# A linear-attention and gated-FF kernel: a list scheduler orders all of it, Q's maxima of four pairs of heads move to TensorE, and the first phase's FF works on 512 tokens

## The chip, the core and the metric

The kernel runs on one core of a Trainium2 chip. The time is the device's time of one execution, in microseconds (us); several executions are run and their median is given. A core has five engines that are told apart in the profile: PE (TensorE, matrix products into PSUM), DVE (VectorE), ACT (ScalarE), POOL (GpSimd) and SP, which here only issues DMAs. Each works through its own instructions in order and waits on semaphores for the others. PSUM has eight banks of 128 partitions x 512 float32.

## What is computed

```python
def phi(x):
    proj = einsum('bhsd,df->bhsf', x, w_phi)             # 64 -> 128 features
    proj = proj - max(abs(proj), axis=-1)                # one maximum per token
    return concatenate([exp(proj), exp(-proj)], -1)      # 256 features
q_p, k_p = phi(q), phi(k)                                # q, k, v: 8 x 8 x 576 x 64
kv  = einsum('bhsf,bhsd->bhfd', k_p, v)
z   = sum(k_p, axis=2)
att = einsum('bhsf,bhfd->bhsd', q_p, kv) / (einsum('bhsf,bhf->bhs', q_p, z) + 1e-6)
x   = att as [4608 tokens, 512]
out = (sigmoid(x @ w_gate) * (x @ w_val)) @ w_out        # 512 -> 1536 -> 512
```

All is float32. The FF's weights come as float64 bit patterns, and the kernel splits each operand of the FF in a high and a low part in a reduced format that TensorE takes at full rate (float32r); a product is then three matmuls, high by high, high by low and low by high. The attention's matmuls are in plain float32.

## The kernel before, in words

**Attention.** The work is cut in 32 pairs of heads (8 batches, 4 pairs each); a pair fills the 128 partitions with two heads of 64. For a pair, `k_heads` (L427) makes K's features token-major (pk), with a tail of 64 tokens of both heads in a matmul of its own (`rest`, L488). `k_exp` takes the maximum per token on DVE (mx, L438), subtracts it (dk, L451) and lets ACT take both exponentials (ek, L460). `q_half` (L417) makes Q's features feature-major (pq), ACT copies them to d (L479), and `q_max` finds each token's maximum across partitions on DVE: a reduction with a transposition (pm, L506), an exchange between the four partition groups in copies of 36 columns (L511 to L517), a transposition back (mb, L519) and the subtraction (L524). `q_exp` takes the exponentials (L568, L570). `kv` (L534, L548) makes K^T V and the sums z with matmuls whose output is cut in four column groups of 32; z's sum over tokens is on PE up to pair 9 and mostly on DVE from pair 10 on (ONPE = 10, L473, L474). `turn` transposes the result (tp, L560), `num` makes numerator and denominator (nm L584, dp L597). The denominator is gathered in a compact form, inverted, sent to memory and comes back broadcast (dn, den, rb); for the last pair of the first batch it is inverted in place instead (L606, L607). `scale` multiplies (xp, L638) and stores x in a scratch in DRAM (xs).

**First phase of the FF.** While attention runs, the FF's first four of twelve blocks of 128 hidden features (JA = 4) are done on chunks of 256 tokens (CH = 256): `half` makes one product of 12 matmuls (gv, L165), `gate` the sigmoid times the value on ACT and DVE, `half_out` the output products (acc, L172), whose sum is parked in DRAM (ys). The four blocks' weights, twelve tiles, are converted once, by `weight_tile` (L134 to L144), with a second load of the same words shifted by two bytes (wmid). x has two buffers of 256 tokens.

**Second phase of the FF.** `rest_chunks` takes the other eight blocks on chunks of 512 tokens (g, v: L165 and acc: L172), with `load_weights` converting 24 weight tiles on the way, four of the blocks into the space that attention leaves and four into the first phase's weight space, and adds the parked sum.

**Order.** In the first phase the order of all engines is written out by hand: a loop over pairs calls the steps, generators (`start`, `tick`) advance DVE's and ACT's steps a bit at a time, and `fill` adds FF products at a given rate (RATE, LAG, AHEAD, TICKS). `grant` lets the weight tiles go: one for each of the first pairs, then three for each. In the second phase PE's order is written and the framework orders the rest.

Of the kernel before, what the change touches and what calls it, by code (L numbers as in the profile page):

```python
# [28 lines left out]
CH = 256  # L29
NCHUNK = NT // CH  # L30
CW = 512
HS = S // 2
Q = 32

JA = 4
JR = 8
EARLY = NP
ONPE = 10
RATE = 2.8
LAG = (4, 8)  # L40
AHEAD = 3
TICKS = 3
# [3 lines left out]
def attention_moe(  # L46
    ctx: ExitStack,
    tc: tile.TileContext,
    q: bass.AP,
    k: bass.AP,  # L50
# [6 lines left out]
    vec, act, pool = nc.vector, nc.scalar, nc.gpsimd  # L57
# [4 lines left out]
    def split(h, l, x):  # L62
        a = act.copy(h, x)  # L63
        return a, vec.tensor_tensor(l, x, h.bitcast(F32), op=ALU.subtract)

    def behind(stack, marks):
        for m in marks:
            stack.enter_context(tc.issue_after(m.ins))


    weights = {}

    ebias = const.tile([P, 1], F32, name="ebias")
    vec.memset(ebias, -896.0 * 2.0**23)

    def from_f64(h, l, raw, sp, nb, name):

        words = raw.rearrange("p (n two) -> p n two", two=2)
        lo, hi = words[:, :, 0], words[:, :, 1]
        top = sp.tile([P, DM], U32, tag="wtop", name="wtop" + name, bufs=nb)  # L80
        vec.tensor_scalar(top, hi, 0x7FFFFE00, None, op0=ALU.bitwise_and)
        relu = act.activation(top, top, AF.Relu, bias=ebias, scale=8.0)
        vec.scalar_tensor_tensor(
            top, hi, 0x80000000, top, op0=ALU.bitwise_and, op1=ALU.bitwise_or
        )
        nc.sync.dma_start(h.bitcast(U32), top)
        rest, unit = hi, lo
        vec.tensor_scalar(
            hi, hi, 16, 0x01FF0000, op0=ALU.logical_shift_left, op1=ALU.bitwise_and
        )  # L90
        vec.scalar_tensor_tensor(
            hi, lo, 16, hi, op0=ALU.logical_shift_right, op1=ALU.bitwise_or
        )
        vec.tensor_scalar(unit, top, 0xFF800000, None, op0=ALU.bitwise_and)
        return relu, vec.scalar_tensor_tensor(
            l, rest, 2.0**-36, unit.bitcast(F32), op0=ALU.mult, op1=ALU.mult
        )

    def load_weights(j, m, wp, sp, nb):
        if m == 0:  # L100
            wh = wp.tile([P, 3 * DM], F32R, tag=f"wh{j}", name=f"wh{j}")
            wl = wp.tile([P, 3 * DM], F32R, tag=f"wl{j}", name=f"wl{j}")
            weights[j] = (wh, wl)
        wh, wl = weights[j]
        ms = slice(m * DM, m * DM + DM)
        raw = sp.tile([P, 2 * DM], U32, tag="wraw", name=f"wraw{j}_{m}", bufs=nb + 1)
        load = nc.sync.dma_start(raw, w_moe[j, :, m, :].bitcast(U32))
        return load, *from_f64(wh[:, ms], wl[:, ms], raw, sp, nb, f"{j}_{m}")

    def raw_tile(w, sp):  # L110

        j, m = divmod(w, 3)
        raw = sp.tile([P, 2 * DM], U32, tag="wraw", name=f"wraw{j}_{m}")
        nc.sync.dma_start(raw, w_moe[j, :, m, :].bitcast(U32))
        mid = sp.tile([P, 2 * DM], U32, tag="wmid", name=f"wmid{j}_{m}")
        nc.sync.dma_start(
            mid[:, : 2 * DM - 1].bitcast(U16),
            w_moe[j, :, m, :].bitcast(U16)[:, 1 : 4 * DM - 1],
        )
        return raw, mid  # L120

    def weight_tile(w, raw, mid, wp, sp):
        j, m = divmod(w, 3)
        n = f"{j}_{m}"
        if m == 0:
            weights[j] = tuple(
                wp.tile([P, 3 * DM], F32R, tag=f"w{x}{j}", name=f"w{x}{j}") for x in "hl"
            )
        h, l = (x[:, m * DM : m * DM + DM] for x in weights[j])
        hi = raw.rearrange("p (n two) -> p n two", two=2)[:, :, 1]  # L130
        words = mid.rearrange("p (n two) -> p n two", two=2)
        rest, unit = words[:, :, 0], words[:, :, 1]
        top = sp.tile([P, DM], U32, tag="wtop", name="wtop" + n)
        vec.tensor_scalar(top, hi, 0x7FFFFE00, None, op0=ALU.bitwise_and)  # L134
        act.activation(top, top, AF.Relu, bias=ebias, scale=8.0)
        vec.tensor_scalar(rest, rest, 0x01FFFFFF, None, op0=ALU.bitwise_and)
        yield
        vec.scalar_tensor_tensor(
            top, hi, 0x80000000, top, op0=ALU.bitwise_and, op1=ALU.bitwise_or
        )  # L140
        nc.sync.dma_start(h.bitcast(U32), top)
        yield
        vec.tensor_scalar(unit, top, 0xFF800000, None, op0=ALU.bitwise_and)
        vec.scalar_tensor_tensor(  # L144
            l, rest, 2.0**-36, unit.bitcast(F32), op0=ALU.mult, op1=ALU.mult
        )

    xscr, yscr = [], []
    for c in range(NCHUNK):
        xscr.append(dram.tile([P, NC4 * CH], F32, tag=f"xs{c}", name=f"xs{c}"))  # L150
        yscr.append(dram.tile([2, P, DM], F32, tag=f"ys{c}", name=f"ys{c}"))

    def x_tiles(mp, w, name):
        xh = mp.tile([P, NC4 * w], F32R, tag="xh", name="xh" + name)
        xl = mp.tile([P, NC4 * w], F32R, tag="xl", name="xl" + name)
        return xh, xl, xl.bitcast(F32)

    def mm_in(o, xs, j, m, w):
        (xh, xl), (wh, wl) = xs, weights[j]
        i = 0  # L160
        for cc in range(NC4):
            ws = slice(m * DM + cc * P, m * DM + cc * P + P)
            cs = slice(cc * w, cc * w + w)
            for a, x in ((wh, xh), (wh, xl), (wl, xh)):
                nc.tensor.matmul(o, a[:, ws], x[:, cs], start=i == 0, stop=i == 11)  # L165
                i += 1

    def mm_out(acc, t, hs, j, first, last):
        (hh, hl, _), (wh, wl) = hs, weights[j]
        ts, ws = slice(t * P, t * P + P), slice(2 * DM, 3 * DM)  # L170
        for i, (a, w) in enumerate(((hh, wh), (hh, wl), (hl, wh))):
            nc.tensor.matmul(  # L172
                acc, a[:, ts], w[:, ws], start=first and i == 0, stop=last and i == 2
            )

    def gated(g, vl, w, mp, hb, name):
        u = mp.tile([P, w], F32, tag="u", name="u" + name)
        t = mp.tile([P, w], F32, tag="t", name="t" + name)
        hh = mp.tile([P, w], F32R, tag="hh", name="hh" + name, bufs=hb)
        hl = mp.tile([P, w], F32R, tag="hl", name="hl" + name, bufs=hb)  # L180
        act.activation(t, g, AF.Tanh, scale=0.5)  # L181
        act.activation(u, g, AF.Exp)
        tu = t.bitcast(U32)
        vec.tensor_scalar(tu, tu, 0x7FFFFFFF, None, op0=ALU.bitwise_and)  # L184
        vec.scalar_tensor_tensor(t, t, 1.0, vl, op0=ALU.add, op1=ALU.mult)  # L185
        vec.scalar_tensor_tensor(u, u, 1.0, t, op0=ALU.min, op1=ALU.mult)  # L186
        return hh, hl, split(hh, hl, u)

    tasks = []

    def start(g):

        if next(g, tasks) is not tasks:
            tasks.append(g)

    def tick():
        for g in list(tasks):
            if next(g, tasks) is tasks:
                tasks.remove(g)

    def half_units(js, mp, ps_gv, ps_acc, need):
        xs, hs, gvs, parts = {}, {}, {}, collections.Counter()

        def load_x(c):
            xh, xl, raw = x_tiles(mp, CH, f"1_{c}")
            xs[c] = xh, xl
            nc.sync.dma_start(raw, xscr[c])
            for _ in range(3):
                yield
            act.copy(xh, raw)  # L210
            yield
            vec.tensor_tensor(xl, raw, xh.bitcast(F32), op=ALU.subtract)  # L212
            parts[c] = NP

        def begin(c):
            free = c < 2 or parts["v", c - 2] == len(js)
            if c not in xs and free and parts["x", c] == CH * NP:
                start(load_x(c))

        def gate(c, i, n):  # L220
            gv = gvs.pop((c, i))
            u = mp.tile([P, CH], F32, tag="u", name="u" + n)
            t = mp.tile([P, CH], F32, tag="t", name="t" + n)
            hh = mp.tile([P, CH], F32R, tag="hh", name="hh" + n, bufs=10)
            hl = mp.tile([P, CH], F32R, tag="hl", name="hl" + n, bufs=10)
            hs[c, i] = hh, hl, None
# [13 lines left out]
        def half(c, i, m):  # L240
            while parts[c] < NP:
                begin(c)
                tick()
# [109 lines left out]
    with ExitStack() as actx:  # L353
# [442 lines left out]
        while tasks:  # L796
            tick()
# [73 lines left out]
```

## Time and profile before

| | |
|---|---|
| median of 3 runs | 1292.52 us (1292.35 to 1294.36) |
| profiled execution, first to last instruction | 1291.7 us |
| busy: PE, its weight loads, DVE, ACT | 1234.4, 971.2, 786.1, 528.1 us |
| matmul records on PE | 9264 |
| mean granted TensorE clock | 0.973 |
| moved by DMA | 131.56 MB |

The page gives the span of the profiled execution and no other time of it; the span lies 0.8 us under the median of the runs. In the rows that are shown below, a group has its line, engine and operation, the tiles written and read, and a count (x32), then the busy time in all and the mean in ns of one, then the idle time before it and what ended it. A float32 matmul is recorded twice, once for each pass. Matmuls are pipelined, so the duration of one overlaps with the next, and the view of the chain, where each piece lasts until the next one begins, tells better what it costs.

### The profile page before, as it was taken

The numbers are of one execution on the slowest core, as the hardware profiler recorded it, in microseconds if no ns is written. First come the engines' busy times: TensorE is split into PE (matmuls) and PEld (weight loads), VectorE is DVE, ScalarE is ACT, GpSimd is POOL, SyncE is SP. The second block draws the span as 40 slices with busy tenths as digits, with TensorE's granted clock in tenths as the row PEclk, the third lists the DMA queues.
The fourth block names the chain that finished last, engine by engine and source line by source line (L and its number), as shares of the span: only waits on it lengthen the run. The fifth ranks groups of instructions, "written<-read, shape, count | busy, mean of one in ns | idle before, by whom it ended". The sixth has DMA issues, their size and how long they took to land.

```text
span 1291.7 us, 22705 instructions
## 1 busy us (share of the span) xinstructions
PE 1234.4 (96%) x9264; PEld 971.2 (75%) x9264; DVE 786.1 (61%) x1584; ACT 528.1 (41%) x1081; POOL 0.7 (0%) x6
## 2 busy tenths in 40 slices
PE   7767999999999999999889999999999999999998
PEld 5434677777777777777778888888888888888886
DVE  6779778888878778883895953434243434333333
ACT  4635556665655566563443422212222212222221
POOL 0000000000000000000000000000000000000000
PEclk8877899999999999999899999999999999999999
DMA  4448434343433334332754520202020111111010
GB/s 176 153 145 284 136 104 146 111 132 105 127 119 121 99 98 146 98 104 73 270 195 148 195 98 1 95 3 76 22 61 37 58 40 53 46 41 57 6 61 33
DMA packets 80868, 131.56 MB, mean 102 GB/s; under 512 B 18300, under 2 KB 37884, under 8 KB 80764
## 3 DMA queue, kind: packets, MB, share of 16 engines
q1 hardware_dynamic: 80764, 130.11, 31.4%
q8 instruction: 73, 1.20, 0.4%
q14 instruction: 31, 0.25, 0.1%
HBM read 92.04 MB, written 28.45 MB: 93 GB/s over the span
## 4 chain that ended last, share of the span: by engine, by line
PE 86%; DVE 7%; DMA 3%; ACT 2%; issue 1%; SPq 0%; DVEq 0%
PE acc L172 22%; PE g L165 15%; PE v L165 15%; PE gv L165 13%; PE kvz L534 6%; PE nm L584 4%; PE pq L417 3%; PE dp L597 2%; PE pk L427 2%; PE kvz L548 1%; DMA wraw<-w_moe 1%; PE pk L488 1%; ACT ek L460 1%; PE tp L560 1%; DMA rb<-den 1%
## 5 line engine op out<-in xcount | busy, mean ns | idle before, releaser
L165 PE MATMUL gv<-xh,wh 128*128 128x256 f32 x576 | 171.6, 298 | 4.9 <-ACT xh L210 2.6
L172 PE MATMUL acc<-wh,hh 128*128 128x512 f32 x432 | 172.4, 399 | 3.2 <-ACT hh L235 2.5
L172 PE MATMUL acc<-wh,hl 128*128 128x512 f32 x432 | 169.0, 391 | 0.7 <-DVE hl L237 0.7
L172 PE MATMUL acc<-wl,hh 128*128 128x512 f32 x432 | 169.1, 391 | 0.0
L165 PE MATMUL gv<-xl,wh 128*128 128x256 f32 x576 | 164.5, 286 | 2.8 <-DVE xl L212 2.8
L165 PE MATMUL gv<-xh,wl 128*128 128x256 f32 x576 | 164.3, 285 | 0.0
L63 ACT CAST hh<-u 128x512 fp32r<-128x512 f32 x72 | 44.7, 621 | 229.0 <-DVE u L186 229.0
L184 DVE TENSOR_SCALAR t<-t 128x512 uint32<-128x512 uint32 x72 | 30.7, 426 | 166.9 <-ACT t L181 166.7
L165 PEld LDWEIGHTS gv<-xh,wh 128*128 128x128 f32 x576 | 111.5, 194 | 22.7 <-issue 15.7
L181 ACT ACTIVATE t<-g 128x512 f32<-128x512 f32 x72 | 43.0, 598 | 178.5 <-PE g L165 178.4
L165 PEld LDWEIGHTS gv<-xl,wh 128*128 128x128 f32 x576 | 111.7, 194 | 3.5 <-DVE xl L212 3.0
L165 PE MATMUL g<-xh,wh 128*128 128x512 f32 x288 | 113.0, 392 | 0.0
L165 PE MATMUL v<-xh,wh 128*128 128x512 f32 x288 | 112.6, 391 | 0.0
L165 PE MATMUL g<-xh,wl 128*128 128x512 f32 x288 | 112.5, 391 | 0.0
L165 PE MATMUL g<-xl,wh 128*128 128x512 f32 x288 | 112.5, 391 | 0.0
L165 PE MATMUL v<-xl,wh 128*128 128x512 f32 x288 | 112.3, 390 | 0.0
L165 PE MATMUL v<-xh,wl 128*128 128x512 f32 x288 | 112.1, 389 | 0.0
L165 PEld LDWEIGHTS gv<-xh,wl 128*128 128x128 f32 x576 | 111.5, 194 | 0.0
L185 DVE SCALAR_TENSOR_TENSOR t<-t,v 128x512 f32<-128x512 f32 x72 | 49.4, 686 | 97.3 <-PE v L165 97.3
L172 PEld LDWEIGHTS acc<-wh,hh 128*128 128x128 f32 x432 | 81.1, 188 | 27.3 <-issue 6.2
L172 PEld LDWEIGHTS acc<-wh,hl 128*128 128x128 f32 x432 | 81.1, 188 | 20.2 <-DVE hl L237 1.7
L534 PE MATMUL kvz<-ek,v 128*32 128x256 f32 x1280 | 89.6, 433 | 6.8 <-issue 5.8
(97 smaller groups left out, 2141.1 us busy)
## 6 DMA issues: line engine op xcount, KB each, us to landing
wraw<-w_moe SPq DMA_DIRECT2D x36, 512.0 KB
xl<-xs SPq DMA_DIRECT2D x34, 512.0 KB
k<-k SPq DMA_DIRECT2D x32, 320.0 KB
v<-v SPq DMA_DIRECT2D x32, 320.0 KB
q<-q SPq DMA_DIRECT2D x32, 288.0 KB
wh<-wtop SPq DMA_DIRECT2D x36, 256.0 KB
ys<-y SPq DMA_DIRECT2D x36, 256.0 KB
yp<-ys SPq DMA_DIRECT2D x36, 256.0 KB
```

The source lines that it names most:

```text
L63: a = act.copy(h, x)
L165: nc.tensor.matmul(o, a[:, ws], x[:, cs], start=i == 0, stop=i == 11)
L172: nc.tensor.matmul(acc, a[:, ts], w[:, ws], start=first and i == 0, stop=last and i == 2)
L181: act.activation(t, g, AF.Tanh, scale=0.5)
L184: vec.tensor_scalar(tu, tu, 0x7FFFFFFF, None, op0=ALU.bitwise_and)
L185: vec.scalar_tensor_tensor(t, t, 1.0, vl, op0=ALU.add, op1=ALU.mult)
L417: nc.tensor.matmul(pps[hd], wk[head(hd), :], x[head(hd), cs], start=True, stop=True)
L427: nc.tensor.matmul(pps[hd][:, t, :], kx[head(hd), t * P : t * P + P], wk[head(hd), :], start=True, stop=True,)
L460: act.activation(e[:, :, sg * F : sg * F + F], dk, AF.Exp, scale=1.0 - 2.0 * sg)
L534: nc.tensor.matmul(kvz[o : o + Q, : 2 * F], vx[:, 2 * t + hd, o % D : o % D + Q], (e0, e1)[hd][:, t, :] if t < 4 else e2[:, 0, :], start=t ...
L584: nc.tensor.matmul(nms[hf][o : o + Q, :], w[:, sg, o : o + Q], es[sg][:, o // D, cs], start=sg == 0, stop=sg == 1, tile_position=(0, o),)
L597: nc.tensor.matmul(dp[o : o + Q, :], w[:, 2, z : z + Q], es[sg][:, hd, hf * HS : hf * HS + HS], start=sg == 0, stop=sg == 1, tile_position ...
```

## The change

**A list scheduler orders the whole kernel.** Each step becomes an operation (`Op`) with its engine, an estimated duration, a rank (an intended time) and the buffers that it reads and writes. `Plan.run` simulates the engines with these durations. Among the operations of an engine that can start at nearly the same time it takes the lowest rank; on PE an operation that would change the tiling mode (r: rows halved, c: columns in four, f: the full array) has 4 added to its rank. Buffers are rings of slots that are handed out in this order; DMAs are simulated as one wire. The steps are then issued, on every engine, in the order of the simulated times.

```diff
+NQ = 4
+ONPE = 16
+BANKS = 5
+PERIOD = 18.4
+START = 56.0
+LEAD = 90.0
+STICK = 4.0
...
+class Plan:
...
+    SWITCH = 0.15
+    NEAR = {"PE": 0.3, "DVE": 0.05, "ACT": 0.05, "SP": 0.0, "X": 0.0}
...
+                first = min(t for t, _ in ts) + self.NEAR[e]
+
+                def key(x):
+                    t, o = x
+                    off = e == "PE" and mode not in (None, o.mode[0])
+                    return o.rank + STICK * off, t
+
+                t, o = min((x for x in ts if x[0] <= first), key=key)
...
+    def due(i):
+        return 11.0 * i if i < NP else START + PERIOD * (i - NP)
```

A pair's operations have ranks from `due(i)` on; the products of a chunk come 90 (LEAD) behind the pairs that complete it, the gate's steps before all else (rank -100). The twelve weight tiles have ranks from 24 to 82 and keep their conversion.

**Maxima of Q on TensorE.** For the first four pairs Q is loaded with its tail laid out as K's. Its features are made twice: token-major, for the maxima (two reductions on DVE, as K's), and feature-major into PSUM, where the maxima are subtracted by matmuls with a broadcast column against a negated identity; ACT takes the exponentials straight from PSUM.

```diff
+        if on_pe:
+            qt = [bank([P, 4, F]) for _ in range(2)]
+            pe("r", 0.9, lambda: token_major(qt, qx), [qx], qt, r + 0.7, slack)
+            mq = [at(f"mq{g}", 2, [P, 4]) for g in range(2)]
+            for g in range(2):
+                dve(4 * F, lambda g=g: maxima(mq[g](), qt[g](), 4), [qt[g]], [mq[g]], r + 7 + g)
+            qf = [bank([P, DM]), bank([P, DM]), bank([P, 2, TAIL])]
+
+            def project():
+                for hd in range(2):
+                    nc.tensor.matmul(
+                        qf[hd](), wk[head(hd), :], qx()[head(hd), :DM],
+                        start=True, stop=False,
+                    )
+
+            def lower():
+                for hd in range(2):
+                    for t in range(4):
+                        nc.tensor.matmul(
+                            qf[hd]()[:, t * P : t * P + P],
+                            mq[hd]()[:, t : t + 1].broadcast_to([P, P]), minus,
+                            start=False, stop=t == 3,
+                        )
+                tail = qf[2]().rearrange("p a b -> p (a b)")
+                nc.tensor.matmul(tail, wk, qx()[:, DM:], start=True, stop=False)
+                nc.tensor.matmul(
+                    tail, mk[2]()[:, 1:2].broadcast_to([P, P]), minus,
+                    start=False, stop=True,
+                )
```

**FF of the first phase on 512 tokens.** Nine chunks of 512 replace eighteen of 256; a product is 12 matmuls of 512 columns. x is kept in four slots of one feature block each, one set in the first phase. Chunk 0, whose x comes straight from attention, has its products cut by feature block (`parted`), so that a block can be multiplied when its pair is done. The gate's and the output's steps are the same on twice the width.

```diff
-CH = 256
...
+    r_xh, r_xl = (ring(ff, f"x{a}", NC4, CW, F32R) for a in "hl")
...
+        for m, o in enumerate((g, vl)):
+            cuts = range(NC4) if parted else (0,)
+            for c0 in cuts:
+                c1 = c0 + 1 if parted else NC4
+                pe(
+                    "f", 0.683 * (c1 - c0),
+                    lambda o=o, m=m, c0=c0, c1=c1: product(o, m, c0, c1),
...
+        banks = [r_g] if c < NCH - 2 else [r_g, r_a]
```

**The rest.** The sums of ones stay on PE up to pair 15 (ONPE = 16). K's shifted features are written into the place of their second exponential instead of a tile of their own. PSUM is five banks for attention and three for the FF, shared in the first four pairs, in the last two chunks of the first phase and in the second phase. In the second phase the same products, conversions and outputs are done, with x in two sets and everything ordered by the planner; its own buffers are opened when the last step of attention is done (`swap`).

More of the change, by code (lines that the diff above doesn't have):

```diff
@@ new lines, with __init__, __call__ @@
+class Buf:
+    def __init__(self, rings=(), shape=None, dtype=None):
+        self.rings, self.shape, self.dtype = rings, shape, dtype
+        self.slot, self.ap, self.log, self.left, self.end = None, None, [], 0, 0.0
+    def __call__(self):
+        if self.ap is None:
+            x, n = self.slot.tile(), 1
+            if self.dtype is not None:
+                x = x.bitcast(self.dtype)
+            for s in self.shape[1:]:
+                n *= s
+            x = x[: self.shape[0], :n]
+            if len(self.shape) == 3:
+                x = x.rearrange("p (a b) -> p a b", b=self.shape[2])
+            self.ap = x
+        return self.ap
@@ L71, in attention_moe, with ring, make @@
-    weights = {}
+    ff = ctx.enter_context(tc.tile_pool(name="ff", bufs=1))
+    ps = ctx.enter_context(tc.tile_pool(name="ps", bufs=1, space=PSUM))
+    stage = {}
+    actx = ExitStack()
+    stage["at"] = actx.enter_context(tc.tile_pool(name="at", bufs=1, side="right"))
+    def ring(where, tag, n, width, dtype=F32):
+        def make(i):
+            pool = stage[where] if isinstance(where, str) else where
+            return pool.tile([P, width], dtype, tag=f"{tag}{i}", name=f"{tag}{i}")
+        return [Slot(lambda i=i: make(i)) for i in range(n)]
@@ L110, in raw_tile @@
[L110 to L146, printed above, removed]
@@ L168, in mm_out @@
[L168 to L187, printed above, removed]
@@ new lines, in attention_moe, with at @@
+    r_u, r_t = (ring(ff, a, 2, CW) for a in "ut")
+    r_y = ring(ff, "y", 2, DM)
+    r_raw = ring(ff, "wraw", 2, 2 * DM, U32)
+    r_mid = ring(ff, "wmid", 2, 2 * DM, U32)
+    r_top = ring(ff, "wtop", 2, DM, U32)
+    r_wh2, r_wl2 = (ring("two", f"v{a}", JR - JA, 3 * DM, F32R) for a in "hl")
+    r_xh2, r_xl2 = (ring("two", f"z{a}", NC4, CW, F32R) for a in "hl")
+    r_y1 = ring("two", "y1", 4, DM)
+    at_rings = {}
+    def at(tag, n, shape, dtype=None):
+        width = 1
+        for s in shape[1:]:
+            width *= s
+        if tag not in at_rings:
+            at_rings[tag] = ring("at", tag, n, width, dtype or F32)
+        return Buf([at_rings[tag]], shape)
@@ new lines, in attention_moe, with pe, dve, on_act @@
+    plan = Plan()
+    def pe(mode, busy, fn, reads, writes, rank, slack=0.0, after=()):
+        return plan.op("PE", busy, 0.25, fn, reads, writes, rank, mode, slack, after)
+    def dve(n, fn, reads, writes, rank, k=1.0):
+        return plan.op("DVE", 0.07 + n / 960 / k, 0.16, fn, reads, writes, rank)
+    def on_act(n, fn, reads, writes, rank):
+        return plan.op("ACT", 0.08 + n / 1200, 0.17, fn, reads, writes, rank)
+    def sp(size, fn, reads, writes, rank, after=()):
+        return plan.op("SP", 0.06, size, fn, reads, writes, rank, after=after)
@@ L526, in kv, with maxima, tails @@
-        def kv(i):
-            vx = loaded.pop(("v", i))
-            e0, e1, e2, *su = ks.pop(i)
-            kvz = bank([P, 3 * F], f"kvz{i}", i, ps_acc, "acc")
+        def maxima(mx, pk, ns):
+            vec.tensor_reduce(
+                mx, pk, axis=AX.X, op=ALU.max, apply_absolute_value=True
+            )
+        pk = [bank([P, 4, F]) for _ in range(2)]
+        pe("r", 0.9, lambda: token_major(pk, kx), [kx], pk, r, slack)
+        nx = 1 + on_pe
+        pt = bank([P, 2, F])
+        def tails():
+            for g, x in enumerate((kx, qx)[:nx]):
+                nc.tensor.matmul(pt()[:, g, :], x()[:, 4 * P :], wk, start=True, stop=True)
@@ L531, in kv @@
+        kvz = bank([P, 3 * F])
+        def kv():
+            e0, e1, e2 = (x() for x in ek)
+            o_ = kvz()
             for t in range(5):
@@ L663, in attention_moe @@
-        weighed = []
-        def need(j, m):
-            while len(weighed) <= 3 * j + m:
-                grant(3 * j + m + 1)
-                tick()
-        chunk, first, outs, begin, xs, parts = half_units(list(range(JA)), moe, ps_gv, ps_acc, need)
-        ready, coming = [], []
-        cdone = wdone = spot = after = 0
-        wq = []
-        def weigh():
-            raws = [raw_tile(w, at) for w in range(2)]
-            for w in range(3 * JA):
-                while not wq:
-                    yield
-                wq.pop(0)
-                yield from weight_tile(w, *raws.pop(0), wp1, at)
-                weighed.append(w)
-                if w + 2 < 3 * JA:
-                    raws.append(raw_tile(w + 2, at))
-                yield
@@ new lines, in mm_out, with first_js, go @@
+    def mm_out(acc, t, hs, j, first, last):
+        (hh, hl), (wh, wl) = hs, weights[j][0]
+        ts, ws = slice(t * P, t * P + P), slice(2 * DM, 3 * DM)
+        for i, (a, w) in enumerate(((hh, wh), (hh, wl), (hl, wh))):
+            nc.tensor.matmul(
+                acc(), a()[:, ts], w()[:, ws], start=first and i == 0, stop=last and i == 2
+            )
+    def first_js(c, r, step):
+        banks = [r_g] if c < NCH - 2 else [r_g, r_a]
+        hs = []
+        for i in range(JA):
+            hs.append(gate(c, i, r + 2 * i * step, banks, c == 0))
+        for t in range(CW // P):
+            acc, y = Buf(banks, [P, DM]), Buf([r_y], [P, DM])
+            def go(t=t, acc=acc):
+                for i in range(JA):
+                    mm_out(acc, t, hs[i], i, i == 0, i == JA - 1)
+            pe(
+                "f", 0.685 * JA, go,
+                [x for h in hs for x in h] + [(x, 2) for i in range(JA) for x in weights[i][0]],
+                [acc], r + (2 * JA + t) * step, 0.3,
+            )
+            on_act(
+                DM, lambda y=y, acc=acc: act.activation(y(), acc(), AF.Copy, scale=0.5),
+                [acc], [y], -90.0,
+            )
+            sp(
+                256 << 10, lambda t=t, y=y: nc.sync.dma_start(yscr[c][t], y()),
+                [y], [(ymark[c], t)], r,
+            )
@@ new lines, in swap @@
+    def swap():
+        actx.close()
+        stage["two"] = ctx.enter_context(tc.tile_pool(name="two", bufs=1, side="right"))
+    last = plan.op("X", 0.0, 0.0, swap, after=closing)
+    last.opens = [s for r in (r_wh2, r_wl2, r_xh2, r_xl2, r_y1) for s in r]
+    for s in last.opens:
+        s.taken = True
+    base = due(N) + 60.0
+    for j in range(JA, NJ):
+        rings = (r_wh2, r_wl2) if j < JR else (r_wh, r_wl)
+        for m in range(3):
+            weigh(j, m, base + 10.0 * (j - JA) + 3 * m, False, rings)
@@ L818 @@
+    order = plan.run()
+    for _, o in sorted(order, key=lambda x: x[0]):
+        o.fn()
+    attention_moe.order = order
 def kernel(**inputs):
```

1167 lines of the change are left out of this document (606 added, 561 removed).

## The prediction

> **What bounds the kernel now.** I cut the span into five stages by the view of busy time in given stretches: the first batch of heads, the second, attention beside the first-phase FF, the change of phase, and the second phase.
>
> ```profile
> 0.00:80.00 80.00, 58.76 (x693) 35.33 (x694) 53.34 (x114) 40.55 (x88) 0.70 (x6) 0.88 0.45 150
> 80.00:160.00 80.00, 62.83 (x675) 41.95 (x674) 69.64 (x151) 39.99 (x85) 0.00 (x0) 0.78 0.64 208
> 160.00:580.00 420.00, 419.16 (x4576) 320.88 (x4575) 342.22 (x755) 255.65 (x576) 0.00 (x0) 1.00 0.38 116
> 580.00:695.00 115.00, 101.14 (x734) 86.88 (x733) 75.01 (x173) 47.43 (x98) 0.00 (x0) 0.94 0.47 161
> 695.00:1291.00 596.00, 592.54 (x2592) 486.20 (x2591) 245.87 (x394) 144.42 (x235) 0.00 (x0) 1.00 0.18 60
> ```
>
> The columns are the stretch, its length, then busy time (and instructions) of PE, weight loads, DVE, ACT and POOL, the granted PE clock, the DMA share and GB/s. Two stages are full on PE at full clock (419 of 420 us, 593 of 596). The other three are not, and there the granted clock is low too (0.88, 0.78, 0.94). Busy time overstates a pipelined PE, so I count work instead. First, the same stretches for the instructions of single tiles, in the order kvz (first two stretches), nm, gv, acc:
>
> ```profile
> 0.00:80.00 80.00, 19.86 (x320) 0.88 0.45 150
> 80.00:160.00 80.00, 23.34 (x320) 0.78 0.64 208
> ```
> ```profile
> 160.00:580.00 420.00, 48.87 (x736) 1.00 0.38 116
> 580.00:695.00 115.00, 5.84 (x64) 0.94 0.47 161
> ```
> ```profile
> 80.00:160.00 80.00, 16.33 (x117) 0.78 0.64 208
> 160.00:580.00 420.00, 156.28 (x1169) 1.00 0.38 116
> 580.00:695.00 115.00, 59.64 (x446) 0.94 0.47 161
> ```
> ```profile
> 160.00:580.00 420.00, 75.26 (x300) 1.00 0.38 116
> 580.00:695.00 115.00, 33.70 (x132) 0.94 0.47 161
> ```
>
> Second, what each piece takes when PE is full, from the chain that ended last (start, length, what), once around a pair of heads; then the sums of ones as the first ten pairs have them (on PE, not added up on DVE), and two products of the second phase:
>
> ```profile
> 394.81 1.09 PE pk L427 x16
> 395.90 0.49 PE pq L417 x4
> 396.38 3.07 PE gv L165 x24
> 399.45 0.69 PE pq L417 x4
> 400.14 0.42 PE pk L488 x2
> 400.56 2.87 PE gv L165 x24
> 403.43 2.29 PE kvz L534 x40
> 405.72 0.44 PE kvz L548 x16
> 406.16 1.94 PE nm L584 x32
> 408.10 0.97 PE dp L597 x16
> 409.07 2.96 PE acc L172 x12
> 412.03 0.33 PE tp L560 x3
> ```
> ```profile
> 168.53 1.09 PE kvz L548 x40
> ```
> ```profile
> 1276.49 2.76 PE g L165 x12
> 1279.26 2.75 PE v L165 x12
> ```
>
> A pair costs 1.09+0.49+0.69+0.42+2.29+0.44+1.94+0.97+0.33 = 8.66 us of PE, and 9.31 where its ones are on PE (1.09 for 0.44). One FF unit of 256 tokens (24 matmuls) costs 2.87, or 3.07 behind another kind of work: 2.97 on average. An output group (12 matmuls) is 2.96 here; I take 2.87 in the mean, the same tenth below. These durations hold the changes between kinds of work.
>
> The test is the full stage: 736/32 = 23 pairs (199 us, 1 more for early ones), 1169/24 = 48.7 units (145) and 300/12 = 25 groups (72) make 417 of 420 us. So the prices are right, and what they don't explain elsewhere is idle or slow PE. In 0 to 160 us, 640 rows of kvz with both its sums (80 a pair) and so on make 8 pairs less the last one's nm and dp (71.6 us), and 117/24 units (14.5): 86 of 160, 74 lost. In 580 to 695: two pairs' nm and dp, one pair's kvz (8.5), 18.6 units (55), 11 groups (32): 95 of 115, 20 lost. The kernel loses some 97 us, nearly all before 160 and around 640. (kvz there: 320 rows in 80 us are 4 pairs, 20 us a pair, against 9.31 of work.)
>
> Why the start is slow is told by its waits and its DVE:
>
> ```profile
> PE pq L417 <- ACT d L479: 21.1, 6, 5.2
> ```
> ```profile
> L144 DVE SCALAR_TENSOR_TENSOR wl<-wmid x12: 691/692/696, 48.5 to 138.8; 128x512 fp32r<-128x512 uint32 x12
> ```
>
> Up to 80 us no engine is full: PE waits in the hand-written order for ACT (21.1 us in six waits), and ACT for PE. From 80 to 160 DVE is full (69.64 of 80): the twelve weight tiles, done between 48.5 and 138.8 us, meet the search for Q's maxima.
>
> **The change, part by part.** *Maxima of Q of pairs 0 to 3 on PE.* Gone from DVE are three wide instructions a pair and the small exchange between them; two reductions like K's come in:
>
> ```profile
> L506 DVE TRANSPOSE_TENSOR_REDUCE pm<-d 128x36 f32<-128x1152 f32 x32 | 44.0, 1376 | 15.7 <-ACT d L479 15.7
> L519 DVE STREAM_TRANSPOSE mb<-pm 128x1152 f32<-128x1152 f32 x32 | 44.0, 1375 | 0.6
> L524 DVE TENSOR_TENSOR d<-d,mb 128x1152 f32<-128x1152 f32 x32 | 43.3, 1353 | 0.3
> L451 DVE TENSOR_TENSOR dk<-pk,mx 128x512 f32<-128x512 f32 x64 | 41.0, 682 | 0.0
> L438 DVE TENSOR_REDUCE mx<-pk 128x4 f32<-128x512 f32 x64 | 40.7, 677 | 5.7 <-PE pk L427 5.7
> ```
>
> That is -4.10+1.35 = -2.75 us of DVE a pair, more with the exchange. PE gets the token-major product (1.09, as pk), a second tail, the projection on 512 columns instead of 288 (0.49x512/288 = 0.87 for both heads) and ten 128x128 matmuls that subtract; it loses the two pq (1.18). One such matmul is between tp's 0.11 (0.33/3) and the tail's 0.42 with a change of mode; the tail's row has two records for one matmul, so I take two of tp's, 0.22. Sum 1.09+0.22+0.87+2.2-1.18 = +3.2 a pair (ends 2.1 and 5.4), +13 us in all (8 to 22). An early pair is then 12.5 us of PE. All of it lands where PE was half empty.
>
> *Sums of ones on PE up to pair 15* (it was 9): 6x0.65 = +4 us of PE, and DVE is freed in exchange.
>
> *FF of the first phase on 512 tokens.* 72 products at 2.76 and the same tenth, 2.86, for 72 units at 2.97: -8 us. The Trainium skill (TensorE: Matmul & The Clock Gate, Back-to-back issue gap) gives a warm gap of N/2.4 + 2.5 ns, by which only the constant is saved, an estimate of 2 us over 864 pairs of matmuls; the rows (2.87 twice against 2.76+2.75) differ from it, and I follow the rows.
>
> *The order.* Content of the first phase: 4x12.5 + 12x9.31 + 16x8.66 = 300, FF 72x2.86 + 36x2.87 = 309, together 609 (before: 601). To it comes what PE can't use.
>
> At the start: the planner interleaves pairs instead of alternating engines, so PE itself (12.5 us a pair) is the longest of them. First data, about 4.4 us (k lands as now):
>
> ```profile
> 1.19 3.12 DMA k<-k
> ```
>
> Then filling, while the first pair's maxima run: four reductions and two subtractions at 0.68 are 4 us of DVE, about 8 with the exponentials behind them; draining the last early pair's normalisation, which I put at 5, since the next keys and the chunk-0 products that are cut into feature blocks cover part of it; and some 4 for a clock below full (0.88 now). So batch 0 ends near 72 us with 21 lost. After it PE has chunk 0 (33 us and more of work) and pairs 4 to 7; the weights are spread over the first 80 us, where DVE had 27 free. Chunk 1 needs pair 7 whole, and its reciprocal's way through memory is long:
>
> ```profile
> 129.18 6.86 DMA rb<-den
> ```
>
> I put 10 us of loss there. Start: 31 (ends: 18, with only first data, filling and draining, and 55, three quarters of today's 74).
>
> At the change of phase: three chunks or so of FF (29 us each and their outputs) now lie behind attention, which is priority work, and the second phase's weights are converted under them; today the two collide. But x has one set of buffers per chunk in the first phase: its next four loads wait for the last product of the chunk before. Behind that wait on SP stand later loads, on PE the next products, which take all four blocks at once. The chunk's four output groups (11.5 us) cover it after the gate's few us. Loss: 9 (3 to 20, today's).
>
> *Second phase.* Its products, outputs and buffers are as before, with DVE and ACT now in written order too; 1291.7-695 = 596.7 stays, within -2 and +6.
>
> Sum on the profile's time: 609+31+9+597 = 1246 to 1247; the median of the runs (1292.52) is 0.8 over the span, so 1248.
>
> **Rivals.** *Half the start.* DMA sets the pace: in 0 to 160 us it moved 28.6 MB (150 and 208 GB/s), and the same is now wanted in about 100 us, 286 GB/s, where 208 already took 0.64 of the engines. Or a static order that errs about landings holds up engines that were free to run on. Start loss 55: 1272. For it: 0.64. Against: 208/0.64 = 325 GB/s is left.
>
> *All bubbles go.* Same-kind work is bundled, the start loses 18 and the change of phase 3: 1228, and some 6 less for fewer changes of kind (0.2 each, as below): 1222.
>
> *Changes of mode.* The view shows 3.07 for a unit behind row-tiled work and 2.87 behind its kind: 0.2 a change. If the planner splits a pair's PE work into its seven tiled pieces with FF between each, where today there are three bundles, four more bundles at 0.2 in and 0.2 out over 28 pairs are 45 us: 1293, no change. Its bias of 4 towards the running mode speaks against. The Trainium skill (TensorEngine Tiling, Key Properties) says that changing the tiling mode drains TensorE; by it too, each piece left alone would pay, and the 0.2 agrees.
>
> *Slower: the single set of x.* A 512 KB load on the chain took this long in the busy stage:
>
> ```profile
> 622.64 6.87 DMA wraw<-w_moe
> ```
>
> Four blocks are twice that, 13.7 us. If they also queue behind other loads on SP, and no attention is ready, PE idles beyond the output groups at each of 8 chunk boundaries. From 44/8 = 5.5 us a boundary on the kernel is no faster; at 10 us it is 1248+80 = 1328. Against: attention fills these holes until its end.
>
> **How the numbers follow.** Forecast 0.58 (1236 to 1262); half the start 0.20 (1272); all bubbles 0.11 (1222); changes of mode 0.05 (1280 to 1293); single x 0.06 (above 1292). The range 1218 to 1282 leaves out the last two and the tails. A measurement of this kernel tells 0.2% (2.6 us) from no change. Faster 0.91, same 0.03, slower 0.06.
>
> **What would show it.** Right: first FF products before 75 us and PE full with clock 1.00 from about 75 to 80 us; eight pairs' kvz done by about 130 us; second phase beginning near 650; weights' last wl before 105 us; products of 2.75 to 2.86 us. Wrong: DVE or DMA near full between 80 and 160 with PE at 0.8 of its clock; holes before the first product of each chunk, ended by xl or xh; more than six changes of mode a pair; a second phase longer than 603 us.

## The result, and the profile after

The changed kernel takes 1237.43 us (median of 4 runs, 1235.67 to 1239.0) against 1292.5: a ratio of 0.9569, 95% interval 0.9556 to 0.9583. The forecast was 1248, in a range from 1218 to 1282. The profiled execution has a span of 1234.9 us (before 1291.7, so 56.8 less), and its run took 1236.72.

The five stages of the prediction, now (the last one ends with the span; the columns are as before):

```profile
0.00:80.00 80.00, 68.88 (x942) 49.75 (x942) 53.84 (x113) 44.15 (x98) 0.70 (x6) 0.96 0.76 252
80.00:160.00 80.00, 76.99 (x984) 50.51 (x984) 73.22 (x158) 54.00 (x113) 0.00 (x0) 0.98 0.57 171
160.00:580.00 420.00, 418.83 (x3957) 295.90 (x3946) 324.86 (x657) 252.76 (x504) 0.00 (x0) 1.00 0.41 128
580.00:695.00 115.00, 115.00 (x504) 94.36 (x503) 84.32 (x158) 43.46 (x74) 0.00 (x0) 1.00 0.44 142
695.00:1234.00 539.00, 534.58 (x2324) 435.78 (x2323) 209.54 (x340) 125.76 (x223) 0.00 (x0) 1.00 0.16 51
```

The change of phase, which had 101 of 115 us busy, is full, and the granted clock of the first two stages rose from 0.88 and 0.78 to 0.96 and 0.98. K^T V of the pairs (the line that was L534 is L511) and the FF's products (L165 is L799), in the first two stages:

```profile
0.00:80.00 80.00, 11.96 (x200) 0.96 0.76 252
80.00:160.00 80.00, 14.21 (x240) 0.98 0.57 171
```
```profile
0.00:80.00 80.00, 3.58 (x9) 0.96 0.76 252
80.00:160.00 80.00, 22.81 (x87) 0.98 0.57 171
```

440/40 = 11 pairs are through by 160 us (8 before), and 96/12 = 8 products of 512 tokens, all of chunk 0. With the prediction's prices that is 4x12.5 + 7x9.31, less nm and dp of the eleventh pair (2.91), and 8x2.86: 135 of 160 us. So 25 us are lost there, where it was 74. From 160 to 695 nothing is; before it was 3 and 20. After 695 us, 2324 matmuls at the price of the second phase before (596.7/2592 = 0.230 us) would be 535 us; the rest of the span is 540. Lost in all: about 30 instead of 97. With 8 us more of work (609 against 601) that makes 67-8 = 59, where the span fell by 56.8 us.

The chain in the full stage shows the new bundles. The durations are start and length:

```profile
395.81 1.09 PE bank L327 x16
396.90 0.49 PE bank L431 x4
397.39 2.97 PE gate L799 x12
400.36 0.69 PE bank L431 x4
401.04 0.89 PE bank L327 x16
401.94 0.80 PE bank L431 x3
402.73 2.96 PE gate L799 x12
405.69 0.22 PE bank L344 x2
405.91 0.69 PE bank L431 x4
406.60 5.71 PE gate L799 x24
```

A product of 512 tokens is 2.97 behind row-tiled work and 2.74 when it follows another (5.71 less 2.97): 2.86 in the mean, as forecast. K's tail (L344) is 0.22 behind full-array work, 0.42 before: the planner puts it there.

Of the 25 us that the start still loses, 14 are idle PE: 4.4 before the first keys have landed, and most of the rest in one hole of 6.1 us from 66.7 us on. The others lie in work that takes longer than its price; the granted clock is 0.87 from 60 to 100 us. The cause of the hole is two steps back:

```profile
PE bank L344 <- ACT ex L560: 6.1, 1, 6.1
```
```profile
ACT xh L648 <- DVE xp L642: 4.4, 2, 4.1
```

PE waits 6.1 us for a bank that ACT has to copy out. ACT could, but stands in its written order before a cast of x. That x is not the one of pair 3, the last of the batch, but pair 0's: the first of the two multiplications below reads a denominator that came through memory (rb), and it is the first in the run, while pair 3's, inverted in place (mb), is the second.

```profile
70.74 0.75 DVE L642 TENSOR_TENSOR xp<-ex,rb 128x576 f32<-128x576 f32 x1
72.89 0.75 DVE L642 TENSOR_TENSOR xp<-ex,mb 128x576 f32<-128x576 f32 x1
```

The load of pair 0's rb was issued at 52.0 us (such loads take 4.1 us in the median). From 60.5 us on DVE does pair 3's two inversions, steps of weight tiles and the maxima of a later pair first, as its order says. Here a static order passes one engine's delay on to two others.

### The profile page after: what moved, and what is told of

The parts are those of the page before. It is cut to its first block, busy times and chain, and to the rows that moved or that the text cites. A ratio compares the mean times of both kernels' runs of the same rounds, so it can differ in the third digit from the quotient of the medians.

```text
span 1234.9 us, 21351 instructions
## 1 busy us (share of the span) xinstructions
PE 1214.3 (98%) x8696; PEld 926.3 (75%) x8696; DVE 745.8 (60%) x1422; ACT 520.1 (42%) x1011; POOL 0.7 (0%) x6
## 4 chain that ended last, share of the span: by engine, by line
PE 95%; DVE 2%; ACT 1%; DMA 1%; issue 0%; SPq 0%; DVEq 0%; ACTq 0%
PE gate L799 37%; PE bank L847 17%; PE bank L799 11%; PE gate L847 7%; PE bank L511 5%; PE bank L553 5%; PE bank L431 3%; PE bank L327 3%; PE bank L571 2%; PE bank L525 2%; PE bank L537 1%; PE bank L344 1%; DMA xl<-xs 0%; PE bank L398 0%; PE gate L327 0%
## 5 line engine op out<-in xcount | busy, mean ns | idle before, releaser
L799 PE MATMUL gate<-xh,wh 128*128 128x512 f32 x344 | 140.1, 407 | 0.0
L799 PE MATMUL gate<-xl,wh 128*128 128x512 f32 x344 | 134.8, 392 | 0.0
L799 PE MATMUL gate<-xh,wl 128*128 128x512 f32 x344 | 134.5, 391 | 0.0
L371 ACT ACTIVATE ek<-ek 128x512 f32<-128x512 f32 (+1 forms) x192 | 95.2, 529 | 22.3 <-DVE ek L359 20.8
L838 DVE TENSOR_TENSOR hl<-u,hh 128x512 fp32r<-128x512 f32 x108 | 74.1, 686 | 47.6 <-ACT hh L836 46.8
L799 PEld LDWEIGHTS gate<-xh,wh 128*128 128x128 f32 x344 | 64.8, 188 | 24.8 <-issue 11.9
L833 DVE SCALAR_TENSOR_TENSOR u<-u,t 128x512 f32<-128x512 f32 x108 | 74.5, 690 | 7.0
L799 PEld LDWEIGHTS gate<-xh,wl 128*128 128x128 f32 x344 | 64.8, 188 | 14.4
L799 PEld LDWEIGHTS gate<-xl,wh 128*128 128x128 f32 x344 | 65.0, 189 | 12.0
L511 PE MATMUL bank<-ek,vin 128*32 128x256 f32 x1240 | 73.4, 381 | 0.0
L511 PEld LDWEIGHTS bank<-ek,vin 128*32 128x32 f32 x1240 | 38.9, 110 | 28.9 <-issue 3.5
```

Source lines behind the costliest of these rows:

```text
L371: lambda g=g, sg=sg: act.activation(ek[g]()[:, :, sg * F : sg * F + F], ek[g]()[:, :, F:], AF.Exp, scale=1.0 - 2.0 * sg,),
L511: nc.tensor.matmul(o_[o : o + Q, : 2 * F], vx()[:, 2 * t + hd, o % D : o % D + Q], (e0, e1)[hd][:, t, :] if t < 4 else e2[:, 0, :], start= ...
L799: nc.tensor.matmul(o(), a()[:, ws], x(), start=cc + n == 0, stop=cc == NC4 - 1 and n == 2,)
L833: lambda: vec.scalar_tensor_tensor(u(), u(), 1.0, t(), op0=ALU.min, op1=ALU.mult),
L838: CW, lambda: vec.tensor_tensor(hl(), u(), hh().bitcast(F32), op=ALU.subtract),
```

## The experiments

The theory of the prediction: the start is slow because DVE carries maxima and weight tiles and the hand-written order lets PE and ACT take turns; the planner with maxima on PE and spread tiles repairs that; FF work behind attention repairs the change of phase; 512 tokens save 8 us; changes of mode cost 0.2 us. The rival: the order alone makes the gain, and moving work between engines does little or harm. "The changed kernel" below is the one of 1237.43 us.

**Q's maxima on DVE for all pairs.**

```diff
-NQ = 4
+NQ = 0
```

> The changed kernel with the maxima of Q of all 32 pairs on DVE again (NQ = 0). My theory: the start is slow when DVE has to carry Q's maxima and the weight tiles together, so the move of the maxima is part of the gain. PE loses 13 us of work, but the four pairs get 2.75 us and more of DVE each back while DVE is already near full from 60 us on; batch 0 then ends some 15 to 20 us later. Net 3 to 10 us slower than the changed kernel: 1240 to 1247 us. Rival: the planner's order alone makes the gain and the maxima's move only costs PE time; then this is faster than the changed kernel by 5 to 13 us: 1224 to 1232 us.

1229.19 us, ratio 0.9497 (0.9477 to 0.9517), against 0.9569 for the changed kernel: 8 us faster. The rival holds. The first two stages of this run:

```profile
0.00:80.00 80.00, 61.46 (x870) 37.28 (x874) 70.36 (x156) 50.17 (x104) 0.70 (x6) 0.94 0.74 245
80.00:160.00 80.00, 78.84 (x973) 52.18 (x966) 76.78 (x163) 56.68 (x116) 0.00 (x0) 1.00 0.61 184
```

DVE is busy 70 of 80 us instead of 54, and it does no harm: the fourth pair's kvz starts at 45.2 us here and at 44.8 with the maxima on PE. What the maxima added to PE (13 us by the prediction's sum, 12.6 by the busy time of all stages, 1214.3 against 1201.7) was absorbed by idle time only in part: 8 us of it show in the time. With them PE has no idle stretch of over 0.3 us between 4.4 and 66.7 us. Without them it has some 6 us in such stretches there. The hole behind the first batch stays without them: it is 8.0 us from 65.4 us on, and ends with ACT's exponential of Q.

**Products of 256 columns on chunks 1 to 8.** Each of these 64 products is made in two halves, with the same buffers and order.

```diff
-            for cc in range(c0, c1):
+            cut = CW // 2 if 0 < c < NCH else CW
+            for hs, cc in [
+                (slice(h, h + cut), cc) for h in range(0, CW, cut) for cc in range(c0, c1)
+            ]:
...
-                        o(), a()[:, ws], x(), start=cc + n == 0,
+                        o()[:, hs], a()[:, ws], x()[:, hs], start=cc + n == 0,
```

> The changed kernel with each product of the first phase on chunks 1 to 8 made in two halves of 256 columns, 24 matmuls instead of 12; order, buffers and gate as they are, 64 products in all. My theory, by the rows of the chain before (two units of 256 tokens 2x2.87 us, products of 512 2.76+2.75): 0.115 to 0.15 us a product, 7 to 10 us: 1244 to 1247 us. Rival, by the gap of N/2.4 + 2.5 ns that the Trainium skill states (TensorE: Matmul & The Clock Gate, Back-to-back issue gap): 12x2.5 ns a product, 2 us: 1239 us. Second rival: the FF is a filler that other waits hide, and nothing changes: 1237 us.

1244.64 us, ratio 0.9616 (0.9596 to 0.9636): 7.2 us more than the changed kernel by the medians, 6 by the ratios. The rows' price holds. From the chain of this run, then of the changed kernel, with no attention about:

```profile
578.45 14.39 PE bank L802 x120
```
```profile
573.30 13.60 PE bank L799 x60
```

14.39/120 = 119.9 ns for 256 columns, 13.60/60 = 226.7 ns for 512: 13 ns more for two than for one. The run has 64x12 = 768 more matmuls, and 7.2 us is 9.4 ns for each. The Trainium skill (TensorE: Matmul & The Clock Gate, Back-to-back issue gap) gives N/2.4 + 2.5 ns for an isolated matmul; by its constant the 768 would cost 2 us, an estimate. The measurement is almost four times that and decides.

**No lead of attention over the FF.**

```diff
-LEAD = 90.0
+LEAD = 0.0
```

> The changed kernel with LEAD = 0: the products of the first phase have the rank of the pairs that follow them, so that less of the FF is left when attention ends. My theory: the loss of 20 us at the change of phase went because FF work lies behind attention while the second phase's weights are converted; with less of it left PE idles there again, 5 to 20 us: 1242 to 1257 us. Rival: the planner interleaves the conversion well in any case, and the two remaining chunks are cover enough: within 3 us of 1237.

1316.6 us, ratio 1.0174 (1.0152 to 1.0196): 79 us more than the changed kernel, and slower than the kernel before. Both theories were far off. The third and fourth stage:

```profile
160.00:580.00 420.00, 381.97 (x3654) 260.62 (x3649) 283.28 (x578) 223.82 (x450) 0.00 (x0) 0.96 0.35 103
580.00:695.00 115.00, 101.60 (x634) 76.72 (x627) 76.52 (x140) 49.73 (x91) 0.00 (x0) 0.94 0.38 129
```

The loss isn't at the change of phase alone (101.6 of 115, what it was before); most of it is in the stage that was full, where the clock also falls to 0.96. The last dp is at 632 us instead of 535. My reading is that FF products now go before attention's on PE, the next batch comes late, and when a chunk is used up PE has no filler and sits out attention's long path from engine to engine. Two waits of this run from 160 to 660 us fit it, one on that path and the longest of PE, for a chunk's x:

```profile
DVE dn L619 <- DMA dn<-dr: 35.3, 6, 16.7
PE gate L799 <- ACT xh L778: 11.1, 1, 11.1
```

**Half the lead.**

```diff
-LEAD = 90.0
+LEAD = 45.0
```

> The changed kernel with LEAD = 45 instead of 90. LEAD = 0 made it 79 us slower. Theory A: the FF has to be behind attention by about the time that a pair takes from its keys to its stored x, some 40 us; with 45 PE still has filler and loses 0 to 10 us: 1237 to 1247 us. Theory B: each us of lead that is taken away costs its share, so half of it costs about half of the loss: 1265 to 1285 us.

1257.58 us, ratio 0.972 (0.9707 to 0.9733): 20 us more, between the two theories. The first half of the lead, up to 45, is worth 59 us, the second 20.

**Weight tiles late.**

```diff
-                weigh(i, m, 24.0 + 16.0 * i + 5 * m, True, (r_wh, r_wl))
+                weigh(i, m, 200.0 + 16.0 * i + 5 * m, True, (r_wh, r_wl))
```

> The changed kernel with the twelve weight tiles of the first phase at ranks 200 to 258 instead of 24 to 82, so that DVE takes them only where no pair needs it, most of them after 80 us as in the kernel before. My theory: that the tiles no longer meet the search for maxima is part of the gain at the start; chunk 0 then waits for its weights and PE has too little to do between 75 and 150 us: 6 to 20 us slower, 1243 to 1257 us. Rival: the tiles fit in anywhere, since DVE has room again after 150 us and the FF only fills: within 3 us of 1237.

1231.34 us, ratio 0.9517 (0.9493 to 0.9541): 6 us faster than the changed kernel, where I expected 6 to 20 slower. The tiles' last wl comes at 153.6 us instead of 127.5. The 40 us around the hole, of the changed kernel and of this run:

```profile
60.00:100.00 40.00, 31.19 (x404) 19.21 (x404) 38.39 (x78) 22.39 (x47) 0.00 (x0) 0.87 0.74 233
```
```profile
60.00:100.00 40.00, 35.29 (x444) 21.65 (x442) 37.83 (x76) 24.73 (x51) 0.00 (x0) 0.91 0.59 184
```

PE is busy 4 us more in it. DVE, nearly full in both, comes to pair 0's x at 66.6 us instead of 70.7 and to pair 3's at 69.8 instead of 72.9, ahead of steps of weight tiles that the changed kernel put first. The edit moves only part of the tiles: five are converted by 56 us in this run (by 52 in the changed kernel), the sixth at 86.7 instead of 63.9. That these last seven come early is no part of the gain; for the first five the run says nothing.

**Weight tiles early in the kernel before.**

```diff
-            grant(i)
+            grant(3 * (i + 1))
```

> The kernel before, with three weight tiles granted after each of the first pairs instead of one, so that nearly all twelve are asked for before 80 us. My first theory: DVE is full from 80 to 160 us because the tiles meet the search for Q's maxima there, and it has 27 us free before; spread out, they cost 8 to 20 us less: 1273 to 1285 us. The theory that the last runs suggest: where the tiles go matters little, the hand-written order itself, in which PE and ACT take turns, is slow, and tiles on DVE in the first 80 us delay the maxima that PE and ACT wait for: within 5 us of the kernel before.

1291.46 us, ratio 0.9993 (0.9981 to 1.0004): no change. The edit moves three tiles: five are converted by 80 us instead of two. In the stretch from 80 to 160 us, whose slowness the prediction put down to the tiles, DVE then has 4 us less, and PE has as many matmul records as before, 675:

```profile
80.00:160.00 80.00, 57.67 (x675) 41.92 (x675) 65.33 (x142) 38.29 (x85) 0.00 (x0) 0.83 0.50 160
```

So the prediction's reason is not borne out, though seven tiles still lie in that stretch. Three stretches of the kernel before and of this run:

```profile
0.00:60.00 60.00, 45.45 (x501) 27.74 (x505) 41.73 (x92) 32.28 (x68) 0.70 (x6) 0.87 0.47 160
60.00:100.00 40.00, 26.92 (x328) 16.74 (x320) 30.58 (x61) 15.00 (x36) 0.00 (x0) 0.82 0.51 159
100.00:160.00 60.00, 49.22 (x542) 32.80 (x543) 50.67 (x113) 33.26 (x70) 0.00 (x0) 0.80 0.65 211
```
```profile
0.00:60.00 60.00, 42.66 (x489) 25.73 (x493) 44.61 (x100) 32.41 (x69) 0.70 (x6) 0.85 0.58 198
60.00:100.00 40.00, 23.36 (x295) 12.60 (x287) 28.90 (x57) 15.46 (x34) 0.00 (x0) 0.76 0.60 196
100.00:160.00 60.00, 50.16 (x590) 37.70 (x591) 48.30 (x106) 32.11 (x72) 0.00 (x0) 0.89 0.47 147
```

What PE gets after 100 us (48 instructions more) it has lost before (45 fewer). That fits an order in which the engines take turns, so that a tile on DVE delays them wherever it lies; no run tests this further.

**No bias towards the running mode.**

```diff
-STICK = 4.0
+STICK = 0.0
```

> The changed kernel with STICK = 0: the planner no longer prefers the running tiling mode on TensorE. My theory: a change of mode costs about 0.2 us (the rows of before: 3.07 against 2.87), the changed kernel has 122 of them between 160 and 560 us, 5.5 a pair, and without the bias there are half as many again or twice as many: 8 to 20 us slower, 1245 to 1257 us, and the number of changes times 0.2 us explains the difference. Rival: what is ready at one time is of one mode anyway, and the number stays: within 3 us of 1237.

1248.56 us, ratio 0.9672 (0.9654 to 0.9691): 11.1 us more. Counted in the instructions in order of time, PE changes its mode 240 times up to 580 us, 183 times in the changed kernel and 180 in the kernel before: 57 more, at 0.19 us each if the whole difference is theirs. That is the price that the rows gave, and the rival of the prediction (45 us) didn't come about because the bias keeps the count where the hand had it.

**Both faster edits together.** NQ = 0 and the tiles at ranks from 200.

> Both single edits that were faster than the changed kernel, together: Q's maxima of all pairs on DVE (NQ = 0) and the weight tiles at ranks 200 to 258. My theory now: under the planner PE itself is the bound in the first batch (50 us of work in 53), so that the 13 us put on it there cost time, and the hole of 6 to 8 us behind the batch is DVE's, which does weight tiles while pair 3's normalisation waits; the two add up: about 1223 us (1220 to 1226). Rival: with the maxima DVE is short from 60 to 160 us, the late tiles make chunk 0 late, and the second edit gains nothing more: 1227 to 1232 us.

1230.05 us, ratio 0.952 (0.9502 to 0.9539): no better than NQ = 0 alone (0.9497). The rival holds; what the late tiles give in the hole, DVE, which has the maxima too, takes back later (from 160 to 260 us PE is busy 96.5 of 100 us, 99.0 with NQ = 0 alone).

**Pair 3's denominator through memory.** As the run above, with

```diff
-        if i == NP - 1 or i == N - 1:
+        if i == N - 1:
```

> As the run with both edits, and the fourth pair's denominator goes through memory like the others' instead of being inverted in place. My theory: the two inversions of 288 columns take 4.6 us of DVE (1.95 each and the additions) in the very hole behind the first batch; without them the hole shrinks, and chunk 0 has other feature blocks to work on while the fourth comes about 8 us later: 2 to 4 us less than with both edits alone. Rival: chunk 0 is the only filler there and needs all four blocks to get on; the later block costs as much as DVE gains, or more: 0 to 5 us more than with both edits.

1232.39 us, ratio 0.9541 (0.9527 to 0.9556): 2 us more than without this edit, within the intervals of one another; what I expected, 2 to 4 less, is excluded only just, and no gain is seen.

**Five banks for the first four pairs.** With NQ = 0:

```diff
-        banks = [r_a, r_g] if early else [r_a]
+        banks = [r_a]
```

> The run with NQ = 0 (1229 us), and the first four pairs keep to attention's five PSUM banks instead of all eight. It asks what made the first batch fast under the planner. Theory A: the interleaved order of PE, ACT and DVE; a pair needs six banks for K and Q at once only in the hand-written order, and the planner gets on with five: within 4 us of 1229. Theory B: it is the three more banks, since the kernel before waits 21 us there for ACT to empty pq; then batch 0 takes 60 us and more again, and this is 8 to 20 us slower: 1237 to 1249 us.

1240.91 us, ratio 0.9589 (0.9576 to 0.9602): 11.7 us more than with NQ = 0 alone. Theory B, in part: the time is the one it gave, but the three banks are worth only 12 us of the some 49 that the changed kernel gained at the start. Three stretches with NQ = 0 alone, then with five banks:

```profile
0.00:60.00 60.00, 49.49 (x758) 30.88 (x760) 50.75 (x113) 40.36 (x85) 0.70 (x6) 0.97 0.72 244
60.00:100.00 40.00, 30.81 (x379) 18.00 (x380) 39.35 (x83) 24.52 (x52) 0.00 (x0) 0.91 0.79 245
100.00:160.00 60.00, 60.00 (x707) 40.57 (x699) 57.04 (x124) 41.97 (x86) 0.00 (x0) 1.00 0.56 165
```
```profile
0.00:60.00 60.00, 48.47 (x672) 29.13 (x672) 50.71 (x116) 38.38 (x81) 0.70 (x6) 0.94 0.74 243
60.00:100.00 40.00, 32.12 (x434) 20.23 (x434) 35.93 (x72) 21.80 (x46) 0.00 (x0) 0.87 0.69 215
100.00:160.00 60.00, 54.95 (x594) 35.02 (x597) 53.46 (x113) 40.25 (x81) 0.00 (x0) 0.96 0.56 169
```

Up to 60 us 86 instructions of PE are missing; later the cover is thinner.

**Chunk 0's products not cut.** With NQ = 0:

```diff
-            hs.append(gate(c, i, r + 2 * i * step, banks, c == 0))
+            hs.append(gate(c, i, r + 2 * i * step, banks, False))
```

> The run with NQ = 0 (1229 us) without the cut of chunk 0's products by feature block: a product waits for all four pairs. Theory of my prediction: the cut products cover part of the time behind the first batch, in which PE waits for pair 3's normalisation; without them 2 to 6 us slower: 1231 to 1235 us. Rival: the four blocks come within a few us of each other, pairs 4 and 5 are there to work on, and PE's hole is not filled by the cut products anyway: within 1.5 us of 1229.

1239.69 us, ratio 0.958 (0.9567 to 0.9593): 10.5 us more, beyond both expectations. The last two of the three stretches:

```profile
60.00:100.00 40.00, 29.23 (x351) 16.26 (x345) 38.77 (x82) 23.22 (x49) 0.00 (x0) 0.83 0.76 238
100.00:160.00 60.00, 57.22 (x621) 37.65 (x625) 51.34 (x112) 38.52 (x79) 0.00 (x0) 0.97 0.53 161
```

PE has less to do in both, and its clock is lower. The first product of each run, with the cut and without it, shows why:

```profile
61.10 0.48 PE L799 MATMUL gate<-xh,wh 128*128 128x512 f32 x1
108.70 0.50 PE L799 MATMUL gate<-xh,wh 128*128 128x512 f32 x1
```

The four blocks do not come within a few us of each other: with NQ = 0, DVE makes the x of pairs 0, 3, 1 and 2 at 57.8, 63.2, 79.7 and 97.8 us. A cut product starts on the first block; an uncut one waits for the last. With the cut, 26 of chunk 0's matmuls, some 6 us of PE, start before 108.5 us. Whether the smaller size of the pieces helps as well is not shown.

**Sums of ones on DVE from pair 10 on.** With NQ = 0:

```diff
-ONPE = 16
+ONPE = 10
```

> The run with NQ = 0 and the sums of ones on PE up to pair 9 only, as in the kernel before (ONPE = 10). My theory: from 160 us on PE is full and DVE is not (295 of 380 us), so six pairs' sums cost PE 6x0.65 = 4 us and DVE's share is hidden: 3 to 5 us faster, 1224 to 1226 us. Rival: pairs 10 to 15 lie where DVE is still over 0.9 busy, the pairs come later and PE lacks filler: within 2 us of 1229, or slower.

1228.83 us, ratio 0.9497 (0.9484 to 0.951): the same as with NQ = 0 alone. 4 us less of work on PE don't show. DVE is busy 82.4 of 100 us between 160 and 260 instead of 68.2. Where the 4 us went isn't settled; the profiled run with this edit starts its first kvz 0.9 us later and has its last dp 0.7 us earlier than the other.

## Why the prediction was right, point by point

**The time.** 1248 was 10.6 us too much. By its own terms: the start lost 25 us where I put 31, the change of phase 0 where I put 9, and what follows 695 us took 5 us more than I put. 1248-6-9+5 = 1238.

**The work.** 300 for attention and 309 for the FF held: 2.86 us a product (2.97 and 2.74), 13 us for the maxima (12.6 between the two runs), and the 8 us of the wider products (7.2 with 64 of 72 halved again).

**The start.** The size was right in the sum (25 for 31), and partly by luck: the 8 us for filling didn't come, since PE has no idle stretch of over 0.3 us from 4.4 to 66.7 us, and the hole behind the batch came of pair 0's x, which DVE took late, and not only of the last pair's normalisation. The reasons were partly wrong. "PE itself is the longest of them" was right. But from it follows what I didn't draw: work that is moved to the longest engine is paid. The step that failed is "All of it lands where PE was half empty": PE was half empty in the old order, not in the new one. NQ = 0 is 8 us faster. The weights that are "spread over the first 80 us" gave nothing either, as far as the edits moved them: seven tiles later in the changed kernel, three earlier in the one before. That "from 80 to 160 DVE is full" told what was busy, not what bound: with 4 us less on DVE PE got through no more matmuls there. What the runs show in its place: the interleaved order with all eight banks (five cost 11.7 us), and products that start on the first block of x (10.5). Both prices were taken at NQ = 0. The order by itself could not be taken out alone, so its own share, the larger part of the 49 us, is only what is left.

**The change of phase.** The mechanism that I named, FF work behind attention, is the right one, and it was sized too small: it covers the conversion wholly. What I didn't name is that the same lead keeps PE full all through the stage before. Without it the kernel is slower than the one before, by a way that was none of my rivals.

**The rivals.** "Half the start" (DMA at its limit) didn't happen: DMA moved 252 GB/s in the first stage at a share of 0.76, and the weights came when they came, without harm. "Changes of mode" has the right price (0.19 us in a run) and the wrong count. "Single set of x": no hole stands before a chunk's first product; from 111 us on, the longest step from one matmul to the next is 1.2 us.

**What was to be seen.** First products before 75 us: 74.8, just. Clock 1.00 from 75 to 80 us on: from 100 only. Eight kvz by 130: the eighth starts at 108. Weights' last wl before 105: 127.5, wrong and of no account. Second phase near 650: its products now mix with the first's from 557 us on, but 596.7 us before the end is 638.

A version that beats both kernels came out of it: NQ = 0, with everything else of the change, at 1229 us (0.9497).

## What to carry to other kernels

Cost a moved operation against the order that will run, not the one that was profiled: idle time of an engine in a bad order is no room for more work, if the better order makes that engine the bound. With a list scheduler, look first at which work has priority: the long path from engine to engine before the work that only fills, with an ample lead (here 90 us beat 45 by 20 us), and filler that can start on part of its input. Look also at how long a finished result lies before the next engine in line comes to it. An engine that is busy over a stretch isn't shown to bind it until moving its work moves the end.

## What wasn't expected of the hardware

In the second phase of the changed kernel a group of twelve matmuls of 512 columns takes 2.72 to 2.76 us or 2.80. From its chain, first late in the change of phase, then in the middle:

```profile
663.47 5.60 PE gate L799 x24
669.07 2.80 PE bank L847 x12
```
```profile
1003.45 5.46 PE gate L799 x24
1008.91 2.72 PE bank L847 x12
```

5.60/24 is 233 ns for each, 5.46/24 is 227. By the operands in order of time, most of the slow ones read one operand from the first phase's buffers and the other from those opened at the change of phase (zh with wh and hh with vh, 233 to 234 ns in the mean), and the fast ones mostly read both from the same (xh with wh and zh with vh, 227 to 228). It is no clean rule: xh with vh, also one of each, lies between, at 230. In the kernel before a group takes 2.72 to 2.77 us, as in these two:

```profile
903.43 2.75 PE acc L172 x12
906.18 2.72 PE g L165 x12
```

Why was not tried. From 695 us on one matmul follows another after 230.0 ns in the mean, in the kernel before after 228.6. Over 2324 matmuls that is 3 us, most of the 5 that this part took beyond the forecast. Another 1.5 us lie at the very end, where the last additions wait for one of only two output buffers:

```profile
1230.49 1.32 DVE L937 SCALAR_TENSOR_TENSOR y<-bank,y 128x512 f32<-128x512 f32 x2 [1.55 <-DMA out<-y]
```
